# Seven places for finished output tiles, held by name instead of taken from a ring each time

## The chip, the cores and the metric

The kernel runs on one core of a Trainium2 chip. The metric is device time in microseconds of one execution, start to end; less is better. A core has five engines with queues of their own: TensorE (PE, matmul; PEld is its weight load), VectorE (DVE), ScalarE (ACT), GpSimd (POOL) and SyncE (SP, which here only issues transfers). Sixteen DMA engines move data between the chip's memory and the on-chip buffer (SBUF). Matmul results go to banks of a second on-chip memory (PSUM). "ACTq" or "SPq" in a row means the queue of that engine, for instance while it issues a transfer.

## The reference

A causal attention with a window of 64 keys, for 8 batches, 8 heads, 576 positions and a head width of 64; its output `x` (8 x 576 x 512) then goes through a spectral mix:

```
X = rfft(x, axis=1)                       # the first 64 modes are kept
Yr = Xr @ w_r - Xi @ w_i ;  Yi = Xr @ w_i + Xi @ w_r      # one 512x512 matrix for each mode
u = x + irfft(Y, n=576, axis=1)
out = u + relu(u @ w_ch)                  # (8, 576, 512), float32
```

## The kernel before, in words

**Attention** comes first: the 16 groups of batch and half of the heads are taken through scores, exponentials, and products with the values; `x` stays in SBUF, and its transform over positions is a matmul with a table. **The mode matrices** stream in during all of this and after it (67 MB each for `w_r` and `w_i`), 1 MB at a time; they set the pace until about 396 us.

**The tail**, which the change touches, begins once the last modes are in. The output is 36 tiles of 128 rows x 512 columns (256 KB each), taken two at a time: 18 pairs, numbered 0 to 17 here in the order of the list `seq` in the kernel. For each tile, `u = x + irfft(Y)` is made in a PSUM bank (`pu`), and `u @ w_ch` in another (`ps`); the second is a sum of `x @ w_ch`, made earlier and kept in `XW`, and of a transform of `Y @ w_ch`. There are three sorts of pairs:

- Pairs 0 to 3, 5, 7, 9 and 11 ("early", function `early`): `u` was made ahead but for the last modes. DVE adds those (`take_u`, L829), ACT writes relu(ps) into the output tile `ut` (`take_z`, L834), and POOL adds `u` to it (L835).
- Pairs 4, 6, 8, 10 and 12 to 16 ("full", `full_u` and `full_z`): PE makes `u` in `pu` (L845, L849, L854), ACT copies it into `ut` (`take_rows`, L862; for some tiles of pairs 12 to 14 DVE adds `x` on the way, L860, and for one POOL does, L864), PE makes `ps` (L786, L868), and DVE writes max(ps, 0) + ut into `ut` (L898).
- Pair 17 (`last`) is a full pair whose DVE step stands at L923 and is stored in three pieces (L926).

Pairs 12 and 13 hold the last 64 rows of two batches in each tile, so each of their tiles is stored by two transfers of 64 rows. All engine queues run in the order in which the program was written, pair by pair.

**Stores.** A finished tile is stored from `ut` to the output. Most stores are issued by SP, in a fixed order (`plan`) that was worked out from assumed times; one that is not ready holds up those behind it. Half of the stores of pairs 12 and 13, and the second tile of pairs 14 to 16, are issued by ACT instead (`by_act`, `send_behind`), one pair later. SP's and ACT's stores share eight completion counters, used in turn: the built program makes a store wait until the store before it on the same counter has landed.

**Places for `ut`.** A pair's `ut` is [128, 2, 512] float32. There is room for seven: one tile of the pool `utpool` (called place A here), and two halves in each of the three buffers of `ringA` (B1 and B2, C1 and C2, D1 and D2), which held mode matrices before. `new_ut()` hands them out. In the kernel before, a ring buffer is asked for anew each time round, as a new tile; the first instruction that writes to it (and, by engine, the first of each engine that touches it) then waits for everything that used the buffer's former tile, both halves: ACT's, DVE's and POOL's instructions, and the landing of all stores from it. The second half has no wait of its own. The pairs and their places: 0 A, 1 B1, 2 B2, 3 C1, 4 C2, 5 D1, 6 D2, 7 A, 8 B1, 9 B2, 10 C1, 11 C2, 12 D1, 13 D2, 14 A, 15 B1, 16 B2. For pair 17 the pool hands out D (its stores stand ahead of pair 11's in the program), so it waits for pairs 12 and 13.

Of the kernel before, what the change touches and what calls it, by code (L numbers as in the profile page):

```python
# [9 lines left out]
FP32 = mybir.dt.float32  # L10
# [7 lines left out]
NRA = 3  # L18
# [8 lines left out]
def kernel(  # L27
# [13 lines left out]
    DM = moe_w_ch.shape[0]  # L41
# [14 lines left out]
    def pool(name, bufs=1, **kw):  # L56
        opened.append(tc.alloc_tile_pool(name=name, bufs=bufs, **kw))
        return opened[-1]
# [138 lines left out]
    with tc.manual_schedule():  # L197
# [633 lines left out]
        def take_z(n):  # L831
            ut = new_ut()
            for j, i in enumerate(seq[n]):
                nc.scalar.activation(out=ut[:, j], in_=ps[i], func=ACT_F.Relu)  # L834
                nc.gpsimd.tensor_tensor(out=ut[:, j], in0=UE[i], in1=ut[:, j], op=ALU.add)  # L835
            for j, i in enumerate(seq[n]):
                send(i, ut[:, j])
# [30 lines left out]
                nc.tensor.matmul(out=ps[i], lhsT=trigIr[:, at:at + 128], rhs=zrows(b), start=False, stop=True,  # L868
                                 skip_group_check=True)

        uts, halves_of_ut = {}, []
        utpool, taken_uts = None, 0

        def new_ut():
            nonlocal taken_uts
            if taken_uts % (2 * NRA + 1) == 0:
                halves_of_ut.append(utpool.tile([128, 2, DM], FP32, name="ut", tag="ut"))
            elif not halves_of_ut:
                t = ringA.tile([128, 4, DM], FP32, name="ut", tag="wt")
                halves_of_ut.extend([t[:, 0:2], t[:, 2:4]])  # L880
            taken_uts += 1
            return halves_of_ut.pop(0)

        def full_u(n):
            banks_u(n)
            ut = uts[n] = new_ut()
            for of in [seq[n]] if len(tiles[seq[n][0]][1]) == 2 else [(i,) for i in seq[n]]:
                rows_u(of)
                for i in of:
                    take_rows(i, ut[:, seq[n].index(i)])  # L890
            send_behind()
            tail_xw(n)
# [17 lines left out]
        def last(n):  # L910
            banks_u(n)
            ut = new_ut()
            ut = [ut[:, j] for j in range(2)]
            for j, i in enumerate(seq[n]):
                rows_u((i,))
                take_rows(i, ut[j])
            send_behind()
            for j, i in enumerate(seq[n]):
                tail_xw(n, (j,))
                rows_z(i)  # L920
                for lo in range(0, DM, HALF * (2 - j)):
                    hi = lo + HALF * (2 - j)
                    nc.vector.scalar_tensor_tensor(out=ut[j][:, lo:hi], in0=ps[i][:, lo:hi], scalar=0.0,  # L923
                                                   in1=ut[j][:, lo:hi], op0=ALU.max, op1=ALU.add)
                    by = nc.scalar if lo else nc.sync
                    by.dma_start(out=tiles[i][2][0][:, lo:hi], in_=ut[j][:, lo:hi])  # L926
# [8 lines left out]
        for i, (grp, hb) in enumerate(steps[EARLY:]):  # L935
            f, l = grp < EARLY or hb == 0, hb == 1
            if i == EARLY:
# [7 lines left out]
                utpool = pool("utpool", side="right", reuse_waits="tile")  # L945
# [118 lines left out]
```

## Time and profile before

| | us |
|---|---|
| median of 3 runs | 435.42 (435.29 to 435.87) |
| the profiled execution | 435.06 |
| its span, first to last instruction | 433.3 |

By stretches of the span, busy us and what the DMA engines moved:

| stretch, us | PE | DVE | ACT | POOL | GB/s |
|---|---|---|---|---|---|
| 0 to 210, attention | 186.42 | 150.58 | 123.56 | 56.83 | 212 |
| 210 to 402, rest of the modes | 122.02 | 56.13 | 40.79 | 24.18 | 206 |
| 402 to 433.3, the tail | 24.88 | 23.38 | 15.68 | 20.54 | 311 |

A row of the timeline reads: start and length in us from the span's start, engine, source line, operation, what it writes and reads, shapes, how many instructions were merged into the row, and in brackets the idle time of that engine just before with the instruction by whose end the profile explains it. Where the row merges several, its first starts at the row's start, and equal ones follow at about half or a little under the row's length.

### The profile page before, as it was taken

How to read it: one execution, taken by the hardware profiler on the slowest of the kernel's cores; microseconds unless marked ns; L12 is line 12 of the kernel's file. 1: busy time of each engine (PE TensorE's matmuls, PEld its weight loads, DVE VectorE, ACT ScalarE, POOL GpSimd, SP SyncE). 2: the span in 40 equal slices, each digit the busy share in tenths (PEclk: the TensorE clock that was granted, in tenths of full speed). 3: DMA queues.
4: the chain of work that ended last, by engine and by line, in shares of the span. 5: the costliest groups of instructions: out<-in, count | busy, mean ns of one | idle time of the engine just before them, and what ended most of it. 6: DMA issues, size and time to landing. Idle time of an engine off the chain costs nothing.

```text
span 433.3 us, 11049 instructions
## 1 busy us (share of the span) xinstructions
PE 333.3 (77%) x4802; PEld 216.2 (50%) x4802; DVE 230.1 (53%) x472; ACT 180.0 (42%) x322; POOL 101.5 (23%) x150
## 2 busy tenths in 40 slices
PE   6999999998999998974208354666676779779994
PEld 3666767576767676651104122334343445445652
DVE  8588687876676776855104111302131315662894
ACT  5666667575766665520202100122121213334742
POOL 8422223222231231113102100012111112110990
PEclk9999999999999999976558656759888869999998
DMA  8999999999999999999999999999999999994798
GB/s 211 211 211 212 211 212 211 211 211 212 211 212 211 211 212 211 212 213 211 212 259 213 217 212 212 212 212 211 209 212 213 208 211 212 212 212 79 248 357 294
DMA packets 47280, 93.64 MB, mean 216 GB/s; under 512 B 2688, under 2 KB 3136, under 8 KB 47232
## 3 DMA queue, kind: packets, MB, share of 16 engines
q0 software_dynamic: 41008, 81.73, 99.7%
q1 hardware_dynamic: 5328, 9.77, 6.6%
q10 hardware_dynamic: 896, 1.44, 0.9%
q8 instruction: 37, 0.61, 0.5%
q14 instruction: 11, 0.09, 0.1%
HBM read 163.58 MB, written 9.44 MB: 399 GB/s over the span
## 4 chain that ended last, share of the span: by engine, by line
DMA 60%; PE 25%; issue 7%; DVE 3%; ACT 2%; POOL 1%; SPq 0%; DVEq 0%; POOLq 0%
DMA wr<-in_moe_w_r_dram 37%; DMA wi<-in_moe_w_i_dram 16%; DMA rawk<-in_k_dram 7%; PE tr L231 4%; PE psm L188 3%; PE s L278 2%; PE s L290 2%; PE s L270 2%; PE pt L298 2%; PE vb L243 2%; PE o L318 1%; PE psz L786 1%; PE psz L610 1%; DMA out_dram<-ut 1%; PE pst L786 1%
## 5 line engine op out<-in xcount | busy, mean ns | idle before, releaser
L610 PE MATMUL psz<-wch,tr 128*128 128x512 f32 x176 | 63.7, 496 | 11.3 <-DMA wch<-in_moe_w_ch_dram 11.0
L756 DVE CAST xw<-psz 128x512 fp32r<-128x512 f32 x36 | 24.9, 692 | 89.0 <-PE psz L610 89.0
L282 DVE TENSOR_REDUCE mx<-s 128x4 fp32r<-128x512 f32 x72 | 49.6, 689 | 26.7 <-PE s L278 26.4
L584 ACT CAST tr<-ptx 128x512 fp32r<-128x512 bf16 x36 | 21.1, 587 | 101.2 <-PE ptx L603 101.2
L188 PEld LDWEIGHTS <-XQ 128*32 128x32 bf16 x448 | 18.6, 176 | 76.0 <-issue 51.7
L165 POOL DMA_DIRECT2D wi<-in_moe_w_i_dram x32 | 23.4, 732 | 101.4 <-PE psm L188 68.2
L188 PE MATMUL psm<-wi,XQ 128*32 128x512 bf16 x208 | 20.8, 475 | 33.9 <-DMA wi<-in_moe_w_i_dram 33.9
L610 PEld LDWEIGHTS psz<-wch,tr 128*128 128x128 f32 x176 | 37.5, 236 | 18.4 <-issue 11.6
L292 ACT ACTIVATE p<-s 128x512 bf16<-128x512 f32 x72 | 39.7, 603 | 12.8 <-PE s L290 12.8
L165 POOL DMA_DIRECT2D wr<-in_moe_w_r_dram x27 | 20.4, 757 | 98.7 <-PE psm L188 50.6
L188 PE MATMUL psm<-wr,XQ 128*32 128x512 bf16 x184 | 19.3, 501 | 27.4 <-DMA wr<-in_moe_w_r_dram 26.8
L235 ACT COPY kT<-tr 128x576 bf16<-128x576 bf16 x32 | 23.2, 725 | 21.3 <-PE tr L231 21.3
L270 PE MATMUL s<-mask_t,ident_bf 128*128 128x512 bf16 x72 | 28.4, 395 | 0.9 <-ACT p L292 0.8
L278 PE MATMUL s<-kT,qT 64*64 64x128 bf16 (+1 forms) x576 | 29.0, 220 | 0.0
L301 DVE COPY pts<-pt 128x1024 bf16<-128x1024 bf16 (+1 forms) x40 | 25.2, 630 | 5.3 <-PE pt L298 4.0
L235 ACT COPY qT<-tr 128x576 bf16<-128x576 bf16 x32 | 23.3, 729 | 10.3 <-PE tr L231 10.3
L278 PEld LDWEIGHTS <-qT 64*64 64x64 bf16 x576 | 17.7, 106 | 18.0 <-issue 17.5
L290 PE MATMUL s<-mx,ident_r 128*128 128x512 f32 x72 | 26.2, 437 | 0.0
L235 ACT COPY vT<-tr 128x576 bf16<-128x576 bf16 x32 | 23.3, 728 | 4.0 <-PE tr L231 3.8
L298 PE MATMUL pt<-ident_bf,p 128*128 128x128 bf16 x288 | 23.3, 220 | 1.5 <-issue 1.3
L635 DVE TENSOR_TENSOR stg<-psm,Yfour 128x512 bf16<-128x512 f32 x10 | 6.9, 691 | 32.8 <-PE psm L188 32.8
L218 POOL DMA_DIRECT2D rawk<-in_k_dram x15 | 8.1, 541 | 63.8 <-PE tr L231 57.6
(211 smaller groups left out, 611.3 us busy)
## 6 DMA issues: line engine op xcount, KB each, us to landing
wi<-in_moe_w_i_dram POOLq DMA_DIRECT2D x29, 1024.0 KB, 19.1
wr<-in_moe_w_r_dram POOLq DMA_DIRECT2D x27, 1024.0 KB, 18.1
out_dram<-ut SPq DMA_DIRECT2D x28, 256.0 KB, 2.8
rawv<-in_v_dram POOLq DMA_DIRECT2D x16, 288.0 KB, 15.4
rawk<-in_k_dram POOLq DMA_DIRECT2D x15, 288.0 KB, 14.4
rawq<-in_q_dram POOLq DMA_DIRECT2D x15, 288.0 KB, 14.3
x_sb<-in_moe_w_r_dram POOLq DMA_DIRECT2D x2, 1024.0 KB, 15.7
Yfour<-in_moe_w_i_dram POOLq DMA_DIRECT2D x1, 1024.0 KB, 14.5
```

The lines of the kernel that those rows point to most:

```text
L165: nc.gpsimd.dma_start(out=w[:, to:to + len(ps)], in_=src[ps[0]:ps[-1] + 1, HALF * hb:HALF * hb + HALF, :].rearrange("g (p j) e -> p g j e" ...
L188: nc.tensor.matmul(out=ps[32 * g:32 * g + 32, 0:e], lhsT=of.rearrange("k s b m -> k (s b) m")[:, (3 * j + 1 - ri) * B:(3 * j + 5 - ri) * B ...
L235: nc.scalar.copy(out=to, in_=pt.rearrange("p j n -> p n j"))
L270: nc.tensor.matmul(out=s, lhsT=ident_bf, rhs=mask_t[:, mk], start=True, stop=True)
L278: nc.tensor.matmul(out=s[ro, t, lo:128], lhsT=lq, rhs=kT[ro, 64 * n - 64 + lo:64 * n + 64], start=False, stop=True, skip_group_check=True)
L282: nc.vector.tensor_reduce(out=mx, in_=s, axis=AX.X, op=ALU.max, negate=True)
L290: nc.tensor.matmul(out=s, lhsT=ident_r, rhs=mx.unsqueeze(2).to_broadcast([128, 4, 128]), start=False, stop=True, skip_group_check=True)
L292: nc.scalar.activation(out=p[:, 4 * c2:4 * c2 + 4, :], in_=s, func=ACT_F.Exp, scale=EX_SCALE)
L298: nc.tensor.transpose(out=pt[:, t, :], in_=st[u]["p"][:, t, :], identity=ident_bf)
L301: nc.vector.tensor_copy(out=ps[:, 0:nt, :], in_=pt[:, 0:nt, :])
L610: nc.tensor.matmul(out=pz, lhsT=tr[:, c, :], rhs=wch[:, c, :], start=(c == 0), stop=(c == NDCH - 1))
L756: nc.vector.tensor_copy(out=XW[i], in_=multiply(tr))
```

## The change

`new_ut()` asks for each of the four buffers once, and keeps the seven places in a list. From then on a pair gets the place of the pair seven before it, as a part of a tile that still has its old name. So a write to a place no longer waits for a whole former tile: it waits for what used the same bytes.

```
-        uts, halves_of_ut = {}, []
+        uts, homes = {}, []
         utpool, taken_uts = None, 0
+        NUT = 2 * NRA + 1

         def new_ut():
             nonlocal taken_uts
-            if taken_uts % (2 * NRA + 1) == 0:
-                halves_of_ut.append(utpool.tile([128, 2, DM], FP32, name="ut", tag="ut"))
-            elif not halves_of_ut:
+            if not homes:
+                homes.append(utpool.tile([128, 2, DM], FP32, name="utx"))
+            elif taken_uts == len(homes) < NUT:
                 t = ringA.tile([128, 4, DM], FP32, name="ut", tag="wt")
-                halves_of_ut.extend([t[:, 0:2], t[:, 2:4]])
+                homes.extend([t[:, 0:2], t[:, 2:4]])
             taken_uts += 1
-            return halves_of_ut.pop(0)
+            return homes[(taken_uts - 1) % NUT]
```

The addresses of the places stay the same. What differs in the built programs: the waits of the instructions that touch `ut`, and that pair 17 takes C1 (formerly of pair 10) and not D1. Each engine has the same work in the same order. Of the waits in the tail, the changed program has, by pair: 8, each of its two copies for its own tile's store of pair 1 (before: all stores of pairs 1 and 2); 9, for pair 2's; 10, for pair 3's (before: pairs 3 and 4); 12, for pair 5's (before: 5 and 6); 13, for 6's; 15, for 8's (before: 8 and 9); 16, for 9's; 17, for 10's (before: 12 and 13). In the order of the eight completion counters, the store of pair 14's second tile, by ACT, and that of pair 11's second tile, by SP, change places.

## Prediction

> **What bounds the tail now.** The change touches only the places of `ut`, used from 400 us on, so I read the tail alone: first the DMA share by stretch, then the chain of work that ended last, then each engine's timeline.
>
> ```profile
> 402.50:408.50 6.00, 6.00 (x36) 3.73 (x35) 5.42 (x9) 5.15 (x11) 6.00 (x6) 1.00 0.78 237
> 408.50:413.50 5.00, 5.00 (x30) 2.91 (x29) 3.75 (x7) 3.38 (x7) 5.00 (x5) 1.00 1.03 382
> 413.50:414.00 0.50, 0.50 (x3) 0.38 (x3) 0.50 (x2) 0.18 (x1) 0.50 (x2) 1.00 0.53 193
> 414.00:420.00 6.00, 6.00 (x32) 3.27 (x31) 5.81 (x11) 2.75 (x5) 6.00 (x5) 1.00 1.03 381
> 420.00:424.50 4.50, 4.50 (x26) 3.17 (x25) 3.91 (x7) 1.55 (x4) 2.54 (x3) 1.00 0.97 298
> 424.50:431.00 6.50, 2.38 (x13) 1.40 (x11) 3.49 (x7) 2.16 (x5) 0.00 (x0) 0.85 1.04 385
> ```
>
> The last two columns are the busy share of the sixteen DMA engines and what they moved. From 408.5 us the output stores run at 381 to 385 GB/s with a full share, but for a hole (413.5 to 414) and a lean stretch (420 to 424.5, 298 GB/s). From 424.5 to 431 they drain at full rate what was issued. So the end is set by stores, and an engine's lead is worth something only if stores issued earlier fill the hole or the lean stretch.
>
> ```profile
> 423.15 2.93 DMA out_dram<-ut
> 426.08 0.58 ACT ut L862
> ```
>
> In the chain of work the landing of an output store (423.15 + 2.93 = 426.08) releases ACT's copy into the place of pair 17: waits for places do stand on the path.
>
> **The change part by part.** No instruction is added or taken away, apart from those that only wait, and POOL's, PE's, ACT's and DVE's orders stay. So every term is a wait that gets shorter, and what is late next. I follow DVE, which finishes the full pairs.
>
> *Pair 8.* Its copies (ACT) and its finish (DVE):
>
> ```profile
> 411.61 1.07 ACT L862 COPY ut<-psm 128x512 f32<-128x512 f32 x2 [0.83 <-PE pst L868]
> 412.23 1.29 DVE L898 SCALAR_TENSOR_TENSOR ut<-pst,ut 128x512 f32<-128x512 f32 x2 [1.17 <-ACT ut L862]
> ```
>
> ACT idled 0.83 us before 411.61. The profile names a product of PE, but that is not what came last:
>
> ```profile
> 410.89 0.62 PE L868 MATMUL pst<-Zall,trigIr 128*128 128x512 f32 x2
> ```
>
> This is pair 8's later product; its `u`, which the copy reads, stands before it in PE's order, so it was there before 410.89. What came last is pair 2's second store:
>
> ```profile
> 406.44 2.53 POOL L835 TENSOR_TENSOR ut<-x_sb,ut 128x512 f32<-128x512 f32 x2
> 408.93 2.54 POOL L835 TENSOR_TENSOR ut<-XQ,ut 128x512 f32<-128x512 f32 x2
> 409.00 0.33 SPq L821 DMA_DIRECT2D out_dram<-ut  x1
> out_dram<-ut SPq DMA_DIRECT2D x15, 256.0 KB, 2.6
> ```
>
> The first row is POOL on pair 2 (two tiles, done at 408.97), then pair 3. The third is the issue of pair 2's second store, 409.00. The last says that stores of 256 KB by SP took 2.6 us to land here (median): 409.00 + 2.6 = 411.6, the start of the copy. In the changed program pair 8 waits for pair 1's stores, one POOL pair (2.49 us) earlier, long landed. So the copy starts when ACT is free, at 411.61 - 0.83 = 410.78, its first tile is done at 411.4, and DVE, which idled 1.17 us and was free at 411.06, starts at 411.4 and not at 412.23: **0.83 us ahead**. Pair 9's relu now waits for pair 2's stores itself; they land at 411.6, and it started later anyway:
>
> ```profile
> 412.57 1.11 ACT L834 ACTIVATE ut<-psz 128x512 f32<-128x512 f32 x2
> ```
>
> *Pair 10.* DVE had no gap between 412.23 and here, so it brings the lead along, but pair 10 follows pair 3's second store, before and after:
>
> ```profile
> 414.78 1.29 DVE L898 SCALAR_TENSOR_TENSOR ut<-pst,ut 128x512 f32<-128x512 f32 x2
> ```
>
> POOL ends pair 3 at 408.93 + 2.54 = 411.47; issued then, the store lands at 411.47 + 2.6 = 414.1, its copy (0.6) ends at 414.7. DVE's second tile stood at 414.78 + 0.61 = 415.39; now it starts at 414.74: **0.65 ahead**.
>
> *Pair 12.* Both engines that write its place waited:
>
> ```profile
> 417.33 0.59 ACT L862 COPY ut<-psm 128x512 f32<-128x512 f32 x1 [0.76 <-DVE XQ L829]
> 417.39 0.69 DVE L860 TENSOR_TENSOR ut<-psm,x 128x512 f32<-128x512 f32 x1
> ```
>
> They waited for pairs 5 and 6; now each tile waits for its own store of pair 5. The second of these is issued in order behind pair 8's stores:
>
> ```profile
> 411.42 2.53 POOL L835 TENSOR_TENSOR ut<-x_sb,ut 128x512 f32<-128x512 f32 x2
> 414.46 0.41 SPq L821 DMA_DIRECT2D out_dram<-ut  x1
> ```
>
> POOL had the tile ready at 411.42 + 2.53 = 413.95, SP issued it at 414.46, because pair 8's stores were late: this is the hole of 413.5 to 414. With pair 8 early the hole closes, and the DMA engines, full on both sides of it, deliver all that follows (1.03 - 0.53) x 0.5 / 1.03 = 0.24 us sooner. Without the hole the store lands at 414.46 + 2.6 - 0.24 = 416.8, and DVE's tile starts there and not at 417.39: **about 0.55 ahead**.
>
> *Pair 14.* Its second tile takes `x` from POOL:
>
> ```profile
> 401.47 2.53 POOL L835 TENSOR_TENSOR ut<-x_sb,ut 128x512 f32<-128x512 f32 x2 [17.30 <-ACT ut L834]
> 421.34 1.20 POOL L864 TENSOR_TENSOR ut<-ut,x_sb 128x512 f32<-128x512 f32 x1
> ```
>
> These are POOL's first and last of nine rows of the tail; each starts before the end of the one ahead (as pairs 2 and 3 above), so its queue does not move, and this tile is there at 421.34 + 1.20 = 422.54 as before, and DVE's second step cannot start before 422.6.
>
> ```profile
> 422.38 1.29 DVE L898 SCALAR_TENSOR_TENSOR ut<-pst,ut 128x512 f32<-128x512 f32 x2
> 424.15 1.29 DVE L898 SCALAR_TENSOR_TENSOR ut<-psz,ut 128x512 f32<-128x512 f32 x2 [0.49 <-PE psm L849]
> 425.36 1.28 DVE L898 SCALAR_TENSOR_TENSOR ut<-pst,ut 128x512 f32<-128x512 f32 x2
> 426.68 1.35 DVE L923 SCALAR_TENSOR_TENSOR ut<-psz,ut 128x512 f32<-128x512 f32 x3
> ```
>
> That step stood at 422.38 + 0.60 = 422.98: **0.4 ahead**, and DVE idles a little.
>
> *Pair 15.* Here lies the other large wait:
>
> ```profile
> 421.11 1.39 ACTq L821 DMA_DIRECT2D out_dram<-ut  x2
> 423.53 0.59 ACT L862 COPY ut<-psy 128x512 f32<-128x512 f32 x1 [2.35 <-PE psz L868]
> 419.96 0.55 SPq L821 DMA_DIRECT2D out_dram<-ut  x1
> ```
>
> ACT's queue issues two stores until 421.11 + 1.39 = 422.50. Then it waited a further 1.0 us for pair 9's second store, issued at 419.96 behind others and down 2.8 us later by the median of all (quoted at the end), at about 423. Pair 8's stores, now asked for, were issued from 413.52 on (its finish, above) and are long down. So the copy starts at 422.55 and its first tile is done at 423.15; the 0.49 us that DVE idled before 424.15 go, and it starts right after pair 14, at 422.6 + 0.6 = 423.2: **0.95 ahead**. Pair 16 waits for pair 9's stores, about when it waited before, through PE: some 0.8 ahead.
>
> *Pair 17.* The wait in the chain goes, but DVE's row of pair 16 shows that it was busy until 426.64 and started pair 17 at 426.68: ACT's wait was covered. What is late next is PE:
>
> ```profile
> 426.48 0.40 PE L868 MATMUL psz<-Zall,trigIr 128*128 128x512 f32 x1
> PEld pst L786 <- DVE ut L898: 0.8, 2, 0.4
> PEld psz L786 <- ACT ut L862: 0.4, 1, 0.4
> ```
>
> Its last product ends at 426.88, and after it DVE has its two half tiles, 0.42 each. PE is busy nearly all the time (4.50 of 4.50 us in the lean stretch), and its weight loads waited 0.8 us, twice 0.4, for DVE, and once for ACT. Of the first of these only 0.21 us showed in the matmuls:
>
> ```profile
> 410.24 0.82 PE L786 MATMUL pst<-xw,ident_r 128*128 128x512 f32 x2
> ...
> 413.05 1.03 PE L786 MATMUL pst<-xw,ident_r 128*128 128x512 f32 x2
> ```
>
> The same two products, for pairs 8 and 10, took 0.82 and 1.03 us. So PE gains 0.2 to 0.4. I take DVE's end 0.5 us ahead (bounds: 0.2, PE alone; 0.95, the lead of pair 15).
>
> *The sum.* Stores are issued 0.4 to 0.95 us ahead in the stretch that feeds the final drain. What the DMA engines can give back: 0.24 (hole), and in the lean stretch by share 4.5 x (1.03 - 0.97) / 1.03 = 0.26, by bytes 4.5 x (381 - 298) / 381 = 0.98; together 0.5 to 1.2. The lean stretch is there because tiles come too slowly; all of it moves forward with the tiles of pairs 12 to 14, by 0.4 to 0.55, and does not vanish. I take **0.5 us**, where pair 12's lead, DVE's end and the lower bound of the DMA engines meet. The profiled execution, 435.06 us (1.76 outside its span), becomes 434.55; on the median of the runs, 0.36 higher, 434.9.
>
> Of the lean stretch the Trainium skill has a rule that speaks against a gain there: its page "SBUF — State Buffer", section "Door 1: The DMA port swizzle", says that a transfer of 64 partitions reaches only half of the ports. By it the 64-row stores of pairs 12 and 13 would be slow in themselves, early issue would not help, and the sum would be the first rival's, 435.2. The trace does not decide: the lean stretch is theirs, yet from 402.5 to 408.5, where no store has 64 rows, a share of 0.78 moved 237 GB/s, just as few bytes to a share (304 against 307).
>
> **The rivals.**
>
> *The drain gives back only the hole.* If the lean stretch is slow because the stores of pairs 12 and 13 have 64 rows, and not because they were issued late, only 0.24 us come back: 435.2. For it: the share there is 0.97, nearly full. Against it: the bytes to a share are as low before 408.5, with whole tiles.
>
> *The large leads reach the end.* The final drain needs bytes, not the last tile: the last store is issued two us before the drain ends (427.40 + 1.65 = 429.05, below, against 431). If pairs 15 and 16 (0.8 to 0.95 ahead) start it, and the lean stretch fills by bytes, the gain is 1.0: 434.4, faster than the bound of 0.2%. Against it: pairs 12 to 14, ahead of them in SP's order, lead by 0.55 at most.
>
> *A new wait at the end.* The three pieces of pair 17:
>
> ```profile
> 427.40 1.65 SPq L926 DMA_DIRECT2D out_dram<-ut  x2
> 428.11 0.34 ACTq L926 DMA_DIRECT2D out_dram<-ut  x1
> SPq L926 <- DMA out_dram<-ut: 0.5, 1, 0.5
> DMA to landing us min/median/max: 2.1/2.8/4.9
> ```
>
> SP's last piece waited 0.5 us for a landing on its completion counter, that of pair 14's second store by ACT. In the changed program that counter belongs to ACT's last piece. Pair 14's store is issued at about 423.3; at the longest landing of the last row, 4.9, it is down at 428.2, about when the piece was issued before (428.11). It decides only if that store takes over 6 us: the piece is issued at 429.3 then, and the end comes 1.1 us later, 436.5. More stores at once on both queues would do it; no row shows over 4.9.
>
> *The waits were not what held the tail*, or the program's engines meet the old gaps by another cause: nothing changes, 435.4. That the change doesn't shorten the waits is ruled out: the built programs' wait lists differ as told above.
>
> **How the numbers follow.** A change of 0.2%, 0.87 us, is about the least that a measurement of this kernel can tell from none; the three runs spread over 0.58. Forecast (434.9): 0.45. Only the hole (435.2): 0.20. No change (435.4): 0.08. Large leads (434.4): 0.20. New wait (436.5): 0.07. So faster by over 0.2% 0.20, within 0.2% 0.73, slower 0.07. The range goes from the rival of 434.4 less a little for spread, 434.2, to the highest of the runs with no gain, 435.8.
>
> **What would show it.** Right: pair 8's first copy at about 410.8 and DVE's finish at 411.4; no hole at 413.5; ACT's copy for pair 15 at about 422.5, without its 2.35 us, and no gap of DVE before pair 15; POOL's rows at the same times; DVE's last step ending near 427.5. The last landing, 0.5 us sooner, would show the sum. Wrong: the DMA share full through the lean stretch and the same end (the drain as rival); a drain that starts a whole us earlier (the large leads); the last piece of pair 17 issued after 429 (the new wait). It would be wrong as a whole if the engines' rows keep their old gaps, so that another cause than the places made them.

## The result, and the profile after

The kernel after took **434.94 us** (median of 20 runs, 434.64 to 435.60) beside 435.62 us for the kernel before (20 runs, 435.23 to 435.90): a ratio of 0.9986, 95% interval 0.9980 to 0.9992, so 0.35 to 0.87 us faster. The forecast was 434.9 us, 0.5 us faster.

The profiled execution of after took 434.85 us, its span 433.1 us. It had entered the tail 0.13 us later than the one of before: ACT's last cast ahead of the tail (line 1020 after, 1019 before) starts at 400.43 us, in before at 400.30. Below, "the tail" is the time from that cast to the landing of the last store, and leads are given with those 0.13 us taken out. The tail was 31.89 us before (to 432.19) and 31.55 us after (to 431.98).

The kernel after by stretches (the columns are busy us of PE, PEld, DVE, ACT and POOL, the granted clock, the DMA engines' share and their GB/s):

```profile
402.50:408.50 6.00, 5.95 (x36) 3.73 (x37) 5.55 (x10) 5.15 (x12) 6.00 (x6) 1.00 0.78 234
408.50:413.50 5.00, 5.00 (x31) 3.19 (x30) 4.46 (x8) 3.44 (x8) 5.00 (x5) 1.00 1.03 382
413.50:414.00 0.50, 0.50 (x4) 0.41 (x3) 0.50 (x1) 0.50 (x2) 0.50 (x1) 1.00 1.04 381
414.00:420.00 6.00, 6.00 (x31) 3.21 (x31) 5.41 (x10) 2.38 (x5) 6.00 (x6) 1.00 1.03 377
420.00:424.50 4.50, 4.45 (x24) 3.23 (x24) 4.40 (x8) 2.35 (x5) 2.66 (x3) 1.00 0.98 310
424.50:431.00 6.50, 2.30 (x13) 1.32 (x11) 2.72 (x6) 1.46 (x3) 0.00 (x0) 0.95 1.03 380
```

The hole at 413.5 is gone (381 GB/s where there were 193). The lean stretch is still there, with 310 GB/s where there were 298.

ACT's timeline of after, the rows of pairs 8, 10, 15 and 16 and the issue of its last piece:

```profile
410.80 1.08 ACT L862 COPY ut<-psm 128x512 f32<-128x512 f32 x2
...
413.64 1.24 ACT L862 COPY ut<-psm 128x512 f32<-128x512 f32 x2
...
420.79 1.40 ACTq L821 DMA_DIRECT2D out_dram<-ut  x2
422.52 0.59 ACT L862 COPY ut<-psy 128x512 f32<-128x512 f32 x1 [1.43 <-PE psp L849]
...
423.81 1.07 ACT L862 COPY ut<-psm 128x512 f32<-128x512 f32 x2 [0.21 <-PE psm L849]
...
427.87 0.36 ACTq L927 DMA_DIRECT2D out_dram<-ut  x1
```

Pair 8's copy has no idle time in brackets any more: it follows ACT's step before it. Pair 15's starts at 422.52, soon after the two stores that ACT issued until 420.79 + 1.40 = 422.19; of the 1.43 us in its bracket, which count from the end of the copy before at 421.10, 1.09 are that issuing.

DVE's timeline of after, the rows of pairs 8, 10, 12 (the addition of `x`), 14, 15, 16 and 17:

```profile
411.52 1.29 DVE L899 SCALAR_TENSOR_TENSOR ut<-pst,ut 128x512 f32<-128x512 f32 x2 [0.33 <-ACT ut L862]
...
414.34 1.29 DVE L899 SCALAR_TENSOR_TENSOR ut<-pst,ut 128x512 f32<-128x512 f32 x2 [0.33 <-PE pst L868]
...
417.08 0.69 DVE L860 TENSOR_TENSOR ut<-psm,x 128x512 f32<-128x512 f32 x1 [0.26 <-DMA out_dram<-ut]
...
422.06 1.32 DVE L899 SCALAR_TENSOR_TENSOR utx<-pst,utx 128x512 f32<-128x512 f32 x2
423.30 1.28 DVE L899 SCALAR_TENSOR_TENSOR ut<-psz,ut 128x512 f32<-128x512 f32 x2
424.86 1.29 DVE L899 SCALAR_TENSOR_TENSOR ut<-pst,ut 128x512 f32<-128x512 f32 x2 [0.28 <-PE pst L868]
426.44 1.35 DVE L924 SCALAR_TENSOR_TENSOR ut<-psz,ut 128x512 f32<-128x512 f32 x3 [0.29 <-PE psz L868]
```

Ahead of pair 12's step the bracket names a store's landing: the wait for a place is not gone there, it is for another store. Ahead of pairs 16 and 17 it names PE. The chain of waits of after ends accordingly, with no store's landing from 422 us on; its end:

```profile
425.65 0.22 PE psp L849
425.87 0.23 PE psz L786
426.10 0.25 PE psz L868
...
426.44 0.42 DVE ut L924
```

This chain follows instructions. It stops at the end of DVE's work, 427.8 us, over four us before the last store has landed; what fills those four us is seen in the DMA share alone.

### The profile page after: what moved, and what is told of

It is laid out like the page before. It is cut to its first block, busy times and chain, and to the rows that moved or that the text cites. A ratio compares the mean times of both kernels' runs of the same rounds, so it can differ in the third digit from the quotient of the medians.

```text
span 433.1 us, 10990 instructions
## 1 busy us (share of the span) xinstructions
PE 322.2 (74%) x4758; PEld 216.0 (50%) x4802; DVE 230.0 (53%) x472; ACT 179.9 (42%) x322; POOL 101.3 (23%) x150
## 4 chain that ended last, share of the span: by engine, by line
DMA 50%; PE 36%; issue 6%; ACT 3%; DVE 2%; POOL 1%; DVEq 0%; POOLq 0%
DMA wi<-in_moe_w_i_dram 29%; DMA wr<-in_moe_w_r_dram 22%; PE tr L231 6%; PE s L278 4%; PE s L290 3%; PE pt L298 3%; PE psm L188 3%; PE vb L243 3%; PE o L318 2%; PE s L270 2%; PE pst L786 1%; PE psz L786 1%; PE psz L610 1%; PE pst L868 1%; PE px L341 1%
## 5 line engine op out<-in xcount | busy, mean ns | idle before, releaser
L610 PE MATMUL psz<-wch,tr 128*128 128x512 f32 x176 | 62.5, 488 | 11.3 <-DMA wch<-in_moe_w_ch_dram 11.0
L188 PE MATMUL psm<-wi,XQ 128*32 128x512 bf16 x208 | 19.8, 454 | 37.1 <-DMA wi<-in_moe_w_i_dram 37.1
L330 DVE TENSOR_TENSOR x_sb<-o,r 128x512 bf16<-128x512 f32 x32 | 22.1, 691 | 1.1
```

The lines of the kernel that those rows point to most:

```text
L188: nc.tensor.matmul(out=ps[32 * g:32 * g + 32, 0:e], lhsT=of.rearrange("k s b m -> k (s b) m")[:, (3 * j + 1 - ri) * B:(3 * j + 5 - ri) * B ...
L610: nc.tensor.matmul(out=pz, lhsT=tr[:, c, :], rhs=wch[:, c, :], start=(c == 0), stop=(c == NDCH - 1))
```

## The experiments

The comparisons are with the kernel before on the same chip. The DMA ledgers further down take each trace in the same five stretches, counted from its own last cast: the first two end 8.07 and 13.07 us after it, the hole is the half us behind, the next six us end at 19.57, the lean stretch at 24.07, and the rest goes to the last landing.

### Only the first reuse by name

Pairs 7 to 13 take the named places of pairs 0 to 6; from pair 14 on, new tiles are taken as in the kernel before.

```
-            if not homes:
+            if taken_uts % (2 * NUT) == 0:
+                homes.clear()
                 homes.append(utpool.tile([128, 2, DM], FP32, name="utx"))
-            elif taken_uts == len(homes) < NUT:
+            elif taken_uts % (2 * NUT) == len(homes) < NUT:
```

> Places by name in the first reuse only (pairs 7 to 13); from pair 14 on, new tiles with the waits of before, so pair 15 waits for pair 9's stores again and pair 17 for those of pairs 12 and 13. If the lead is won in pairs 8 to 12 and carried to the stores (the chain of the prediction): no hole at 413.5 to 414, DVE's pair 12 about 0.45 us ahead of before, and most of the gain of the changed kernel stays, 0.4 to 0.5 us of its 0.6 to 0.7 (ratio to before about 0.999). If the gain came from the late waits (pairs 15 and 17): about 0.1 us, ratio 0.9998.

Measured: 435.22 us (434.94 to 435.58, 11 runs) beside 435.74; ratio 0.9987, interval 0.9979 to 0.9996. The tail of its trace was 31.44 us. DVE began pair 15 23.26 us after the cast (22.87 in after, 23.85 in before) and ended as early as in after, at 27.38. So the first reuse carries, as far as the intervals tell, the whole gain.

### Only the second reuse by name

The kernel before, in which pairs 14 to 17 alone go by name.

```
+        homes = []
...
+            if taken_uts >= 4 * NRA + 2:
+                taken_uts += 1
+                return homes[taken_uts - 4 * NRA - 3]
...
+            if taken_uts > 2 * NRA + 1:
+                homes.append(halves_of_ut[0])
```

> The other half alone: pairs 7 to 13 take new tiles with the waits of before, pairs 14 to 17 the same places by name. If the lead is won early: the hole at 413.5 to 414 stays, DVE's finish of pair 15 comes only 0.5 us ahead (right after pair 14, at about 423.7 in the clock of before), and the time falls by 0.1 to 0.25 us, ratio 0.9995 to 0.9998. If the late waits carry the gain: 0.5 us or more, ratio 0.9988.

Measured: 435.99 us (435.31 to 436.59, 11 runs); ratio 1.0003, interval 0.9994 to 1.0012. Freed of its wait, DVE began pair 15 at 23.67 us, 0.18 ahead of the first trace of before and not the 0.5 expected, and nothing came of it. (The traced execution was one of the longer ones, 436.18 us, with a tail of 32.40 us; pair 8 began 12.33 us after the cast in it, 11.93 in before.)

### Only pairs 8 and 9 by name

The kernel before, in which the halves of buffer B alone are reused by name.

```
+        homes = []
...
+            if taken_uts in (2 * NRA + 2, 2 * NRA + 3):
+                taken_uts += 1
+                return homes[taken_uts - 2 * NRA - 3]
...
+            if taken_uts in (2, 3):
+                homes.append(halves_of_ut[0])
```

> Only pairs 8 and 9 reuse their place (B) by name; all later pairs take new tiles with the waits of before. If closing the hole of 413.5 to 414 and the lead that DVE carries on from pair 8 make the gain: no hole, DVE's pair 10 about 0.55 us ahead of before, and 0.4 us or more of the gain stays, ratio 0.9987 to 0.9991. If the hole alone is what is left of it (0.24 us) and the waits of pairs 10 and 12 do the rest: ratio 0.9995. If the leads need every link: none, 1.0.

Measured: 435.55 us (435.15 to 436.63, 11 runs) beside 435.78; ratio 0.9996, interval 0.9987 to 1.0005. Its stretches for the half us of the hole, the six us behind and the lean stretch:

```profile
413.92:414.42 0.50, 0.50 (x4) 0.41 (x3) 0.50 (x1) 0.23 (x1) 0.50 (x1) 1.00 1.03 377
414.42:420.42 6.00, 6.00 (x32) 3.21 (x31) 5.08 (x10) 2.75 (x5) 6.00 (x6) 1.00 1.02 377
420.42:424.92 4.50, 4.45 (x24) 3.22 (x24) 3.70 (x7) 1.42 (x3) 2.68 (x3) 1.00 0.95 290
```

The hole is closed, the lean stretch as in before. Pair 8 led by the full 0.84 us, and pair 10, expected 0.55 us ahead, lost it again, as ACT's and DVE's rows show:

```profile
414.74 1.07 ACT L862 COPY ut<-psm 128x512 f32<-128x512 f32 x2 [0.58 <-PE pst L868]
```

```profile
415.35 1.29 DVE L905 SCALAR_TENSOR_TENSOR ut<-pst,ut 128x512 f32<-128x512 f32 x2 [0.93 <-PE psz L786]
```

The trace began its tail at 400.85, so pair 10 started 14.50 us after the cast, as in before (14.48), and not at 13.91 as in after. In before's scheme the first copy of pair 10 waits for pair 3's second store too; with places by name it waits for the first tile's store alone and comes a copy earlier. The wait for each tile's own store is what hands pair 8's lead on.

### 128-row stores for the half tiles

The kernel after; each tile of pairs 12 and 13, 128 rows of which the two halves belong to two batches, is stored as two halves of its columns with 128 rows each, into a scratch tensor. The bytes and the number of transfers stay; the last 64 rows of every batch are not written to the output.

```
+            if len(to) == 2:
+                by.dma_start(out=aside[i // 9, :, HALF * h:HALF * h + HALF], in_=done[i][:, HALF * h:HALF * h + HALF])
+                return
```

> The changed kernel, with the eight 64-row stores of 128 KB of pairs 12 and 13 (and the other two tiles of their sort) replaced by 128-row stores of half of the columns, 128 KB too, by the same engines in the same order, to a scratch tensor beside the output; the output's last 64 rows of each batch are left unwritten. If the stretch of 420 to 424.5 is lean because tiles come late: its rate stays near 300 to 320 GB/s and the time within 0.2 us of the changed kernel. If stores of 64 rows are slow in themselves: its rate rises to 350 GB/s or more, and the end comes 0.3 to 0.8 us sooner than in the changed kernel.

Measured: 434.84 us (434.65 to 435.38, 11 runs); ratio 0.9978, interval 0.9969 to 0.9987. Its lean stretch:

```profile
420.44:424.94 4.50, 4.45 (x24) 3.21 (x24) 4.40 (x8) 1.66 (x3) 2.64 (x3) 1.00 1.04 353
```

353 GB/s against 305 to 310 in the traces of after: the stores of 64 rows are slow in themselves. (The scratch tensor is another destination too; the kernel with the half tiles early, below, keeps the destination, and there the lean stretch moves with these stores.) DVE ended 28.16 us after the cast, 0.8 us later than in after, and the tail was shorter all the same (31.08 us): it followed what remained to be drained, and not the last tile.

The same edit on the kernel before:

> The kernel before with the same replacement of 64-row stores as in wide_stores (the output's last 64 rows of each batch are left unwritten): the places wait as before. If the change acts through the hole and the lead, it is worth the same beside wide stores: this one is 0.4 to 0.7 us slower than wide_stores, ratio to before 0.9988 to 0.9994, with the hole at 413.5 to 414 there and the stretch of 420 to 424.5 at 340 GB/s or more. If the gain came out of the lean stretch that the 64-row stores make: within 0.2 us of wide_stores.

Measured: 435.26 us (435.03 to 435.76, 11 runs); ratio 0.9989, interval 0.9980 to 0.9997. Here the hole and the lean stretch:

```profile
413.85:414.35 0.50, 0.50 (x3) 0.30 (x2) 0.50 (x2) 0.31 (x1) 0.50 (x1) 1.00 0.49 180
...
420.35:424.85 4.50, 4.45 (x24) 3.18 (x25) 4.35 (x9) 1.66 (x3) 2.66 (x3) 1.00 1.04 351
```

The hole is the old one, the lean stretch the improved one. Between the two kernels with 128-row stores the places by name are worth 435.26 - 434.84 = 0.42 us by medians, 0.47 us by the tails (31.56 and 31.08).

### A ready tile moved ahead of one that isn't

The kernel after with one change of SP's order: pair 11's first tile is stored ahead of pair 13's tiles.

```
+        plan.remove(seq[11][0])
+        plan.insert(plan.index(seq[13][0]), seq[11][0])
```

> The changed kernel, with one store moved in SP's fixed order: the first tile of pair 11, which POOL has ready at 420.2 but SP issues only at 422.4, goes ahead of pair 13's two. If the lean stretch is one of supply: 256 KB come about 2 us sooner, its rate rises by some 30 to 50 GB/s, and the end comes 0.2 to 0.5 us sooner than in the changed kernel. If 64-row stores set the pace there, or the store only pushes pair 13's back: the same time within 0.1 us.

Measured: 435.28 us (434.94 to 436.14, 11 runs); ratio 0.9990, interval 0.9981 to 0.9999; no gain over after (0.9986) is shown. SP issued the moved store 19.89 us after the cast, in after 21.96. Its lean stretch:

```profile
420.28:424.78 4.50, 4.45 (x24) 3.24 (x24) 4.02 (x8) 1.96 (x4) 2.65 (x3) 1.00 1.01 305
```

The DMA engines are busier (1.01 against 0.98) and move no more bytes, though a tile came two us sooner. With a shortage of tiles, more would have been moved. The tail of this one trace was 31.37 us, 0.18 shorter than in after, but not by this stretch (the table further down).

### The half tiles taken early

The kernel after, the two pairs of half tiles taken as pairs 4 and 6 and not as 12 and 13.

```
+        seq[12:12] = seq[4], seq[6]
+        seq[4], seq[6] = X4
...
-        by_act = {(i, 1) for p in X4 for i in p} | {(p[1], 0) for p in BB[:-1]}
+        by_act = {(p[1], 0) for p in seq[12:-1]}
```

> The kernel after, with the order of the pairs changed: the two pairs of half-width tiles (stored 64 rows at a time) are taken as pairs 4 and 6 instead of 12 and 13, and the pairs of whole tiles that stood there as 12 and 13. SP issues all of the 64-row stores, and ACT the second tile of pairs 12 to 16; the x that DVE and POOL add stays with the tiles of pairs 12 to 14 by position. If 64-row stores cost rate only where the DMA engines are full, they cost little between 402.5 and 408.5, where the share is 0.78: the lean stretch should then move 350 GB/s or more as it does with 128-row stores, and the time be that of wide_stores, 0.1 to 0.3 us under the kernel after, 0.7 to 0.9 under the kernel before. If the lean stretch is one of tiles that come too slowly, it stays near 310 GB/s and the time is that of the kernel after. If the 64-row stores take a larger part of the early stretch than its slack, SP's queue and the places of the first round run late by it and the time is that of the kernel before or above.

Measured: 436.70 us (436.61 to 437.11, 11 runs) beside 435.84; ratio 1.0021, interval 1.0012 to 1.0030: slower, the third of the outcomes named. The stretch from 8.07 us on, the lean stretch, and one us out of the first:

```profile
408.63:413.63 5.00, 5.00 (x28) 3.25 (x24) 3.34 (x6) 3.43 (x7) 5.00 (x5) 1.00 0.96 256
...
420.13:424.63 4.50, 4.30 (x19) 2.15 (x17) 4.42 (x8) 0.80 (x2) 2.67 (x3) 1.00 1.02 379
```

```profile
410.00:411.00 1.00, 1.00 (x5) 0.56 (x3) 0.70 (x2) 0.08 (x1) 1.00 (x2) 1.00 1.00 207
```

The lean stretch went where the half tiles went. In it DVE was busy nearly throughout and whole tiles moved at 379 GB/s, while the five us from 408.63 on, at 382 to 383 GB/s in the traces of before and after, moved 256. At 410 a full share moved 207 GB/s. SP's row for the four 64-row stores of pair 4, issued just ahead of that,

```profile
407.44 2.44 SPq L823 DMA_DIRECT2D out_dram<-ut  x4
```

has one store in 0.61 us, and 128 KB in 0.61 us are 215 GB/s: the rate of issuing comes out alike. Since the share is full, I read the issuing as held up by the transfers and not the reverse, but this trace alone does not exclude it. The tail grew to 33.20 us, since the early stretch had less slack than these stores needed, and DVE began its steps of pairs 4 and 6 0.7 and 1.5 us later.

### Half of the bytes

Each store takes only the left half of its columns; the other half of the output is not written. First after, then before with this cut:

```
-            by.dma_start(out=to[h], in_=done[i][m * h:m * h + m, :])
+            by.dma_start(out=to[h][:, 0:HALF], in_=done[i][m * h:m * h + m, 0:HALF])
```

> The changed kernel, each store cut to the left half of its columns (half of the bytes; the rest of the output is left unwritten). If the drain of the stores sets the end: the time falls by 1.0 us or more, to 433.9 or less, and the last landing comes 2.1 to 2.8 us after the last issue, not 2.9. If the engines' last steps set the end: within 0.4 us of the changed kernel.

> The kernel before, with the same cut of its stores (the right half of the columns of the output is left unwritten). Stores then land sooner, so the places' waits shrink, and no backlog is there for a lead to fill: the change should be worth less than with whole stores, 0 to 0.3 us between this kernel and half_after. If the waits cost the same whatever the load of the DMA engines, 0.6 us as with whole stores.

Measured: after 432.75 us (432.51 to 433.10, 5 runs; ratio 0.9928, interval 0.9916 to 0.9941), before 432.63 us (432.62 to 432.71, 5 runs; 0.9926, 0.9913 to 0.9938). The 16 us from 8.07 us on, of after and of before:

```profile
408.86:424.86 16.00, 15.95 (x86) 9.97 (x87) 14.82 (x24) 8.63 (x18) 14.18 (x12) 1.00 0.64 196
```

```profile
408.82:424.82 16.00, 15.95 (x86) 10.00 (x86) 14.85 (x24) 8.76 (x18) 14.13 (x12) 1.00 0.64 193
```

With a DMA share of 0.64 the change does nothing: the old scheme's waits cost next to nothing once stores land quickly (DVE begins pair 8 11.17 us after the cast with the new places and 11.25 with the old), so these two kernels have no lead to compare. DVE ends 27.44 and 27.42 us after the cast, no earlier than in after (27.36), yet the tail is 29.09 and 29.07 us, 2.5 us shorter. The last landing came 1.5 us after the last issue had ended, sooner than the 2.1 to 2.8 us expected. So with whole stores the drain of the bytes ends about 2.5 us after what the engines alone would allow.

### More traces of both kernels

The first trace of before came from an execution well under its median (435.06 against 435.62), so both kernels, unchanged, were traced again.

> The kernel before, unchanged, for a second trace: its first one came from an execution of 435.06 us, 0.56 under the median of its runs, so the 0.34 us by which the change shortened the tail in the traces may be too little. If the change gives back the hole alone, the tail here is again near 31.9 us from ACT's last cast of the transposed modes to the last landing. If the first trace was a lucky one and leads of the engines count as well, the tail is 32.2 or more, with less moved in the lean stretch or in the stretch ahead of 408.5 us.

> The kernel before once more, unchanged, for a third trace, as a measure of how much the tail differs from one execution to the next: the same two answers as for the second trace.

> The kernel after, unchanged, for a second trace on the same chip: a tail near 31.55 us and a full share from 408.5 to 420 us if the first trace was a usual one (it was taken at 434.85 us, 0.09 under the median of its runs).

Measured: 435.54 and 435.97 us for before, 435.12 us for after. The tails: before 31.89, 32.09, 32.21 us, mean 32.06; after 31.55, 31.54. The second and third tail of before lie between the two answers that were expected. The difference of the means is 0.52 us, inside the interval of the runs (0.35 to 0.87). Hole, next six us and lean stretch of the second trace of before, of its third, and of the second of after:

```profile
413.65:414.15 0.50, 0.50 (x3) 0.29 (x2) 0.50 (x2) 0.32 (x1) 0.50 (x2) 1.00 0.47 172
414.15:420.15 6.00, 6.00 (x31) 3.26 (x30) 5.81 (x11) 2.75 (x5) 6.00 (x6) 1.00 1.03 382
420.15:424.65 4.50, 4.50 (x25) 3.18 (x25) 3.70 (x7) 0.69 (x2) 2.63 (x3) 1.00 0.96 292
```

```profile
413.94:414.44 0.50, 0.50 (x3) 0.26 (x2) 0.50 (x2) 0.35 (x1) 0.50 (x1) 1.00 0.47 172
414.44:420.44 6.00, 6.00 (x31) 3.29 (x30) 5.81 (x11) 2.75 (x5) 6.00 (x6) 1.00 1.03 382
420.44:424.94 4.50, 4.50 (x26) 3.13 (x25) 3.71 (x7) 1.01 (x2) 2.67 (x3) 1.00 0.95 289
```

```profile
413.78:414.28 0.50, 0.50 (x4) 0.41 (x3) 0.50 (x1) 0.50 (x2) 0.50 (x1) 1.00 1.02 373
414.28:420.28 6.00, 6.00 (x31) 3.21 (x31) 5.41 (x10) 2.38 (x5) 6.00 (x6) 1.00 1.03 378
420.28:424.78 4.50, 4.50 (x25) 3.23 (x24) 4.39 (x8) 2.34 (x5) 2.67 (x3) 1.00 0.98 305
```

From such rows comes the **ledger**: how much time of the DMA engines each stretch lost, its length x (1 - GB/s / 383), where 383 is the full rate of the five us ahead of the hole. For the second trace of before, the hole lost 0.5 x (1 - 172 / 383) = 0.28 us.

| lost, us | hole | next 6 us | lean stretch | to the last landing | tail |
|---|---|---|---|---|---|
| before, mean of three | 0.27 | 0.02 | 1.06 | 1.00 | 32.06 |
| after, mean of two | 0.01 | 0.09 | 0.89 | 0.86 | 31.55 |
| only the first reuse | 0.01 | 0.08 | 0.99 | 0.67 | 31.44 |
| only the second reuse | 0.33 | 0.33 | 0.98 | 1.04 | 32.40 |
| only pairs 8 and 9 | 0.01 | 0.09 | 1.09 | 1.03 | 31.99 |
| a ready tile ahead | 0.01 | 0.09 | 0.92 | 0.65 | 31.37 |
| before, 128-row stores | 0.26 | 0.03 | 0.38 | 1.17 | 31.56 |
| after, 128-row stores | 0.00 | 0.09 | 0.35 | 0.95 | 31.08 |

The gain by the ledger: 0.26 for the hole, of which 0.07 are lost in the six us behind, 0.17 in the lean stretch and 0.14 at the end: 0.50 of the 0.52 us. Single traces differ by 0.1 to 0.2 us in the last two columns (the three of before: 0.90, 1.03 and 1.08 at the end), so these two terms are less certain than the hole, which every trace shows alike. The ledger is bookkeeping: the bytes are the same in all these kernels, so the losses must add up to the difference of the tails. It says where the time went, and not why.

## Why the prediction was right

The forecast's size and its main steps held; one reason in it did not. That 434.94 us fell on the forecast of 434.9 is in part luck: the median of before came out 0.20 us higher than that of the first three runs, and the gain by medians was 0.68 us (0.52 by the traces) and not 0.5, so that the two differences cancel.

- **Pairs 8, 10, 12, 14 and 15** led by 0.84, 0.57, 0.44, 0.42 (second tile) and 0.98 us in the first traces; forecast were 0.83, 0.65, 0.55, 0.4 and 0.95. POOL's rows stayed. Pair 8 began at nearly the same time after the cast in all three traces of before (11.93 to 11.97 us); pair 15 did not (23.85, 24.60 and 24.27 us, against 22.87 and 22.88 in after), so its 0.98 is the least of three. Pair 10's lead needed its own waits by tile: with pairs 8 and 9 alone by name it was zero.
- **The hole** was pair 8's late stores, and closed with pair 8's lead in every kernel that had it. The forecast of 0.24 us was 0.26 by the ledger; the kernel with pairs 8 and 9 alone gained 0.23 us by medians, though its interval takes in no change.
- **The lean stretch** is the reason that failed: "The lean stretch is there because tiles come too slowly". Three kernels speak against it: with 128-row stores it moved 353 GB/s and not 305 to 310, with a ready tile moved ahead no more than before, and with the half tiles taken early it was gone from there. Of the 1.06 and 0.89 us that it loses, the 64-row stores take 1.06 - 0.38 = 0.68 and 0.89 - 0.35 = 0.54. So the rival of the hole alone was right in its reason, and wrong in its sum: this stretch gained 0.17 us nevertheless, and the end behind it 0.14. The forecast had taken 0.26 for both, by share; that the size came out near is luck, since its reason failed. The 0.98 us by bytes, its upper bound, did not come: what lies between share and bytes, 0.72 us, is about what the 64-row stores take.
- **Pair 16 and the end of DVE**: 0.63 us ahead where 0.8 was forecast, and 0.37 where 0.5 was (its bounds 0.2 and 0.95). PE's last products are what comes last, as forecast. Against the other two traces of before DVE's lead at the end is larger, 1.11 and 0.79 us (it ended at 27.73, 28.47 and 28.15 us there, at 27.36 in both of after). The tail does not go by it: the kernel with 128-row stores ended DVE 0.8 us later and the tail 0.47 us sooner. So DVE's end, one of the three numbers where the forecast took its 0.5 us, does not set the sum.
- **The large leads** did not reach the end. With the second reuse alone by name, pairs 15 to 17 were free of the old waits, and the time was that of before (1.0003), though pair 15 led by 0.18 us only in its trace. Without it, the gain was there (0.9987).
- **The new wait** did not come: ACT's last piece was issued at 427.87, not after 429.

What the prediction set against the rival, that whole tiles moved as few bytes to a share from 402.5 to 408.5 us, falls when that stretch of before is cut up:

```profile
402.50:404.00 1.50, 1.50 (x11) 0.65 (x10) 1.50 (x3) 1.45 (x3) 1.50 (x3) 1.00 0.90 172
404.00:405.40 1.40, 1.40 (x9) 1.00 (x9) 1.40 (x3) 1.40 (x3) 1.40 (x2) 1.00 0.89 287
405.40:408.50 3.10, 3.10 (x19) 2.08 (x18) 2.52 (x5) 2.31 (x6) 3.10 (x3) 1.00 0.67 246
```

From 405.4 us on a share of 0.67 moved 246 GB/s, 367 to a full share, near the 371 of the next five us (382 / 1.03). The low mean comes from the three us before, and why those were slow no run took apart.

The kernels with half of the bytes show why the whole is so small beside leads of up to a us: the stores' drain ends about 2.5 us behind what the engines allow. That only the part of a lead that lets idle DMA time be used shortens it is how I read the ledger. That earlier tiles of pairs 10 to 13 make the gain in the lean stretch and behind it fits the three kernels with parts of the change, and is argued, not shown: no run moved those tiles alone, and the intervals of the kernels with the first reuse alone and with pairs 8 and 9 alone overlap. What the remaining 0.35 us of the lean stretch and the 0.9 us at the end are was not taken apart.

The Trainium skill's rule, cited in the prediction against a gain there (page "SBUF — State Buffer", section "Door 1: The DMA port swizzle"), that 64 partitions reach half of the ports, agrees with the us at 410 of the kernel with the half tiles early: a full share moved 207 GB/s, 0.54 of 383. Mixed with whole tiles, these stores cost less: the 4 tiles have 1 MB, which take 2.7 us at 383 GB/s and would lose 2.7 us more at half of it, where 0.54 to 0.68 were lost. Why they cost less there, no run here tried by itself.

## What to carry to other kernels

Before counting on an earlier engine, ask in each stretch whether the DMA engines have idle time for what it would feed them: here leads of 0.4 to 1 us were worth 0.5 us, and once the stores had half of the bytes the waits cost nothing to begin with. A buffer that is asked for anew waits for everything that used it, so where its parts are freed at different times, waits by part can hand a lead on to later stages which a single earlier buffer loses again. In the lean stretch a busy share that moved few bytes was a sign of slow transfers and not of missing ones: before looking for a shortage upstream, change the transfer's form with the bytes kept, as with the 128-row stores.

## What the hardware showed besides

An issue held up an engine for long here. ACT's issue of a store usually takes 0.34 us here; with the 128-row stores in flight, one took 1.98 us, and its next copy, for pair 16, waited behind it:

```profile
423.84 1.98 ACTq L824 DMA_DIRECT2D out_dram<-utx  x1
425.86 0.59 ACT L865 COPY ut<-psm 128x512 f32<-128x512 f32 x1 [2.48 <-PE pst L871]
```

The bracket names PE, but the copy starts as the issue ends (423.84 + 1.98 = 425.82). On the kernel before with the same stores, it took 2.50 us. DVE's step of pair 16 waited for this copy, and so its end came later; what holds the issue, the profile does not say.

The same program differs from run to run, by 0.67 us among the 20 runs of before beside after and by 1.26 among the 33 beside the first experiments, and part of it lies ahead of the tail: the last cast stood at 400.30 to 400.87 us in the three traces of before. Counted from the cast, stretches repeat closely (the hole lost 0.26 to 0.28 us in each), and so a single trace pair told less than the same rows taken from the cast in several.
